# Adding the stored tiles back by blocks of channels, and keeping four tiles on chip

## The chip, the core and the metric

The kernel runs on one core of a Trainium2 chip, as one launch. The metric is the device time in microseconds (us), the median of three runs; beside them stands one execution under the hardware profiler, from which all rows below come. The core's engines are TensorE (PE), VectorE (DVE), ScalarE (ACT), GpSimd (POOL) and SyncE (SP), which here only issues transfers; 16 DMA engines move the bytes.

## What is computed

The output is x + A + B, for 2048 positions (16 tiles of 128) and 448 channels, in 32-bit floats. A is a long causal convolution along the positions, gated by the normalized input; B picks, for each position and each of 16 heads, two of 4096 experts, gathers their rows and sums them.

```
xn = layernorm(x)
# A: a short shift convolution, times v, then a causal convolution as long as the sequence
kv = shift4(k, shift_k) * v
y  = irfft(rfft(kv, 4096) * rfft(ssm_k, 4096))[:2048] + kv * ssm_D
A  = xn * y
# B: scores from xn, the two best experts of each head, a softmax g over them
act = gelu(einsum("nd,nhkd->nhk", xn, u[top_e]))
B   = einsum("nhk,nhk,nhkd->nd", g, act, v[top_e])
out = x + A + B
```

## The kernel before

**Experts.** The 16 position tiles T are worked through in order, each in eight batches, 128 batches in all. A batch is four gathers of 128 rows of 3584 bytes (`gather`, L582, issued by POOL) into one of five slots of `ring`; the product with the position's row on DVE (`prod`, L615, 2 us); four sums on ACT (L621) and a gelu (L623); the coefficients `co` and `cc` (L629, L628), on POOL for the first 104 batches and on DVE for the last 24; and the weighted sum of the four gathered slots on PE into the accumulator `pv` (`val`, L634). After a tile's eighth batch ACT adds the mean and writes the tile from `pv` to the staging tile `fo` (`fold`, L658), and SP stores `fo` to the output (`store`, L662).

**Convolution.** It is a Fourier transform in three steps over groups of four channels. Part 0 holds groups 0 to 27 (channels 0 to 111), part 1 groups 28 to 111 (channels 112 to 447). `conv_in` (L705, L709) transforms to 33 frequencies q; `spectrum` and `inverse` (L756, L773, L801, L820, L824) multiply and go back, frequency by frequency, with the two transforms' real and imaginary columns in `x1b`, a buffer of 84 groups by 33 q by 8 columns. The inverse writes its 17 results over q 0 to 16; the columns of q above 16 are not read again once `spectrum` has read them. `conv_out` ("out0" for part 0, "out1" for part 1) finishes seven groups at a time: seven transposes of `x1b` (`psz`, L842), a copy by ACT (`zt`, L844), seven small matmuls (`fin`, L849) into a PSUM bank, and the gate on DVE, which multiplies by `XA`, the normalized input (L860 for the tiles already done, in place in `XA`; L865 for later ones, into `G`). "out1" has twelve such blocks of 28 channels.

**Why tiles come back.** When tile T is folded before the convolution of its channels is ready, its sum lacks A. "out0" lies behind tile 8 and "out1" behind tile 14. So tiles 0 to 8 lack all of A, and tiles 9 to 14 lack the channels of part 1; tile 15 gets A as a matmul of `G` into `pv` (L652). After the last gate the kernel of before loads tiles 0 to 14 from the output into `x1b` (L1003, from here called read-backs), adds `XA` (L1005, one add per tile) and stores them again (L1006).

**What sets the order.** The program is a list of operations with keys (planned times). A planner in the kernel file (`Plan.solve`) runs a simple model of the engines and takes, on each engine, the ready operation with the lowest key; what it writes out is then the fixed order of each engine. `RANK` is a table that adds, for each kind of operation, four numbers to the keys (interpolated over the kernel's length), and so shifts kinds against each other everywhere. A gather also waits for a PE instruction that the plan put half a us ahead of it. SP issues its transfers strictly in its order.

```python
    join([("x1q", 1, i) for i in range(17)] + ["out_in"], ["fb"])
    for T in range(0, T_OUT1):
        ...
        op("DVE", dve(D - c), lambda T=T, c=c, w=w: nc.vector.tensor_add(second["x1b"][:, w], second["x1b"][:, w], XA[:, T, c:]), ...)
        i = op("SP", 0.08, lambda T=T, c=c, w=w: nc.sync.dma_start(out[T][:, c:], second["x1b"][:, w]), ...)
```

Of the kernel before, what the change touches and what calls it, by code (L numbers as in the profile page):

```python
# [93 lines left out]
class Plan:  # L94
# [133 lines left out]
    "SPwq": (-10.5, 7.5, -46.0, -13.5), "SPx": (92.5, 175.0, 250.5, 125.0), "co": (-183.5, -76.0, -185.5, -457.5),  # L228
    "coef": (-230.5, -356.5, -140.5, -235.5), "ds": (149.0, 210.5, 206.5, 283.0), "es": (64.0, -136.0, 8.5, -185.0),
    "fin@out0": (-90.0, -32.0, -52.5, -95.0), "fin@out1": (-172.5, -183.0, -139.5, -189.5), "flag": (53.5, 83.5, 133.0, 121.0),  # L230
    "fold": (-199.5, -258.0, -262.5, -275.0), "gat": (-151.0, -139.0, 56.5, 85.5), "gate@out0": (-26.0, -26.0, -8.0, -27.5),
    "gate@out1": (-101.5, -201.0, -216.5, -140.0), "gateG@out0": (-31.5, -31.5, -46.0, -85.5), "gateG@out1": (51.5, 33.0, 83.0, 92.0),
# [860 lines left out]
```

## Time and profile before

| what | us |
|---|---|
| median of three runs (906.52, 906.61, 910.87) | 906.61 |
| the profiled execution | 912.46 |
| its span, first to last instruction | 910.7 |
| PE, DVE, ACT, POOL busy | 701.0, 676.3, 569.5, 590.6 |
| mean share of the 16 DMA engines busy by gathers / by SP's transfers | 74.4% / 13.4% |
| last product of the experts (L615) ends | 890.1 |
| last matmul of the transforms (L849) ends | 892.4 |
| read-back adds (L1005) | 893.7 to 901.1 |

The profiled execution lies 5.85 us above the median, 1.75 us of which are outside its span. No engine is busy throughout: the busiest has 77% of the span. In the stretches from 125 to 800 us the DMA engines are busy 84 to 97% and POOL issues a gather every 1.25 us where nothing holds it. The last 20 us look otherwise: the gathers are over, and what runs is the end of the transforms, the adds and the stores. That end is what the change rewrites.

A view of stretches gives, for each stretch of the span, the busy time of each engine (with its instructions), the granted TensorE clock (1.00 is 2.4 GHz, 0.50 is 1.2 GHz), the share of the DMA engines and the GB/s. A timeline row is start, duration, engine, line, operation, tiles and shapes, count, and in brackets the idle time before it with what ended it.

### The profile page before, as it was taken

Reading aid. Unit: us, or ns where it says so; the run is one execution under the profiler, and the core shown is the slowest. Engines: PE = TensorE matmul, PEld = TensorE weight load, DVE = VectorE, ACT = ScalarE, POOL = GpSimd, SP = SyncE. Lnnn points to the kernel's source line nnn. Section 1 sums busy time; section 2 is a strip of 40 time slices with the busy share of each in tenths; the row PEclk is TensorE's granted clock in tenths of the full one; section 3 lists DMA queues with packets and bytes.
Section 4 is the critical chain, followed back from the end, with each engine's and each line's share of the span. In section 5 each row is a group of like instructions: output and inputs, shape, how many; then the busy total and the mean of one; then the engine's idle time right before and its main releaser. Section 6 shows DMA issues by size and latency. Waiting matters only on the chain. (4 is left out here: it accounts for less than half of the span.)

```text
span 910.7 us, 14005 instructions
## 1 busy us (share of the span) xinstructions
PE 701.0 (77%) x4100; PEld 409.5 (45%) x4100; DVE 676.3 (74%) x1577; ACT 569.5 (63%) x1874; POOL 590.6 (65%) x740
## 2 busy tenths in 40 slices
PE   4887786986879868869788865676778878878683
PEld 1434454553545546546456544453433333335451
DVE  2678879878877887787988867667698888874444
ACT  2579764447557656765755666447688887775551
POOL 0156578777776776777777777847777776655630
PEclk9998789998988998998999787778898999996955
DMA  9996688888998998899989899988998999988984
GB/s 370 375 409 235 211 298 282 295 286 297 320 310 293 323 320 272 300 334 311 307 305 350 303 337 326 355 288 280 328 336 301 326 311 341 305 299 278 350 318 150
DMA packets 60054, 280.77 MB, mean 308 GB/s; under 512 B 10304, under 2 KB 21056, under 8 KB 59712
## 3 DMA queue, kind: packets, MB, share of 16 engines
q0 software_dynamic: 40960, 234.91, 74.4%
q1 hardware_dynamic: 19008, 44.87, 13.4%
q8 instruction: 34, 0.56, 0.2%
q14 instruction: 52, 0.43, 0.1%
HBM read 272.98 MB, written 6.77 MB: 307 GB/s over the span
## 5 line engine op out<-in xcount | busy, mean ns | idle before, releaser
L582 POOL DMA_INDIRECT ring<-in_uv_dram,idx x512 | 505.7, 988 | 277.1 <-issue 93.0
L621 ACT ACTIVATE ring<-ring 128x448 f32<-128x448 f32 x512 | 288.7, 567 | 56.6 <-DVE ring L615 29.5
L615 DVE TENSOR_TENSOR ring<-ring,xs 128x1792 f32<-128x1792 f32 x128 | 257.4, 2014 | 71.7 <-DMA ring<-in_uv_dram,idx 50.9
L634 PE MATMUL pv<-ring,cc 128*32 128x448 f32 x1024 | 144.3, 642 | 83.2 <-POOL cc L628 49.4
L482 DVE MAX8 SC<-bank 128x8 f32<-128x64 f32 x512 | 118.6, 232 | 45.7 <-PE bank L477 8.9
L705 PE MATMUL bank<-c,S 128*64 128x132 f32 x896 | 82.8, 340 | 27.2 <-ACT ring L621 12.9
L621 ACT ACTIVATION_READ_ACCUMULATOR ring<-ring 128x1 f32 x512 | 97.2, 190 | 0.0
L473 PE MATMUL bank<-WR,xh 128*128 128x512 f32 x192 | 86.9, 453 | 10.3 <-issue 3.6
L705 PEld LDWEIGHTS bank<-c,S 128*64 128x64 f32 x896 | 66.2, 171 | 62.0 <-ACT ring L621 27.5
L634 PEld LDWEIGHTS pv<-ring,cc 128*32 128x32 f32 x1024 | 21.9, 115 | 133.4 <-POOL cc L628 66.2
L475 PE MATMUL bank<-WR,xl 128*128 128x512 f32 x192 | 78.8, 411 | 0.5 <-DVE xl L462 0.5
L474 PE MATMUL bank<-WR,xh 128*128 128x512 f32 x192 | 78.8, 410 | 0.3 <-DVE WR L432 0.3
L709 ACT ACTIVATE x1b<-bank 128x264 f32<-128x264 f32 x84 | 31.2, 386 | 45.7 <-PE bank L705 38.2
L473 PEld LDWEIGHTS bank<-WR,xh 128*128 128x128 f32 x192 | 38.8, 202 | 41.7 <-issue 15.6
L756 PE MATMUL bank<-x1b,S 128*128 128x336 f32 x132 | 49.9, 489 | 9.1 <-issue 3.9
L489 DVE FIND_INDEX8 SC<-SC,bank 128x8 uint32<-128x256 f32 x128 | 52.5, 423 | 0.0
L688 DVE TENSOR_TENSOR S<-S 128x1024 f32<-128x1024 f32 x28 | 34.6, 1234 | 24.2 <-PE bank L705 16.2
L773 DVE TENSOR_TENSOR S<-bank,S 128x224 f32<-128x224 f32 (+1 forms) x66 | 40.8, 619 | 13.8 <-ACT S L767 6.7
L628 POOL TENSOR_TENSOR cc<-sm,c 128x128 f32<-128x128 f32 x104 | 46.4, 447 | 2.6
L849 PE MATMUL bank<-c,S 128*128 128x64 f32 x168 | 33.2, 357 | 12.9 <-ACT S L844 10.5
L849 PEld LDWEIGHTS bank<-c,S 128*128 128x128 f32 x168 | 29.4, 261 | 29.9 <-ACT S L844 18.5
L475 PEld LDWEIGHTS bank<-WR,xl 128*128 128x128 f32 x192 | 38.1, 199 | 10.3 <-DVE xl L462 1.2
(137 smaller groups left out, 1047.3 us busy)
## 6 DMA issues: line engine op xcount, KB each, us to landing
R<-in_wq_dram SPq DMA_DIRECT2D x16, 896.0 KB
S<-in_kvh_dram SPq DMA_DIRECT2D x28, 400.0 KB
ring<-in_uv_dram,idx POOLq DMA_INDIRECT x512
S<-in_fq_dram SPq DMA_DIRECT2D x32, 128.0 KB
out_dram<-fo SPq DMA_DIRECT2D x16, 224.0 KB
...
```

What stands on the lines that cost most here:

```text
L473: nc.tensor.matmul(o, xh[:, c, :], wh[:, c, ns], start=(c == 0), stop=False)
L474: nc.tensor.matmul(o, xh[:, c, :], wl[:, c, ns], start=False, stop=False)
L475: nc.tensor.matmul(o, xl[:, c, :], wh[:, c, ns], start=False, stop=False)
L482: nc.vector.max(mx[:, 8 * n + j, :] if safe else m2[:, m, 2 * j:2 * j + 8], bank[s.i][:, 64 * j:64 * j + 64])
L489: nc.vector.max_index(m4i[:, 2 * m + g, :], m2[:, m, 8 * g:8 * g + 8], bank[s.i][:, 256 * g:256 * g + 256])
L582: g = nc.gpsimd.indirect_dma_start(dst, None, uv, bass.IndirectOffsetOnAxis(ap=idx[:, T % 8, r, j:j + 1], axis=0)).ins
L615: op("DVE", dve(m * D), lambda: nc.vector.tensor_mul(U[:, :m, :], U[:, :m, :], xs[:, :m, :D]), r=["xs"], w=u[:m], key=k, name="prod")
L621: op("ACT", 0.575, lambda r=r: nc.scalar.activation(U[:, r, :], U[:, r, :], AF.Copy, accum_out=aw[:, r:r + 1]), w=[u[r], ("aw", b % 4, r)] ...
L634: v = nc.tensor.matmul(pv[32 * r:32 * r + 32, :D], cc[b % 3][:, r, :], ring[:, b % RING, r, D:], start=(j == 0), stop=(j == NB - 1), tile_ ...
L705: nc.tensor.matmul(o[64 * i:64 * i + 64, w * j:w * j + w], src, f1[:, i, :], start=True, stop=True, tile_position=(0, 64 * i))
L756: op("PE", 0.95 * n / 448 + 0.05, lambda t=t, sl=sl: nc.tensor.matmul(bank[sl.i][:, :n], fm, x1[p][:, :, q, t, :], start=True, stop=True), ...
L849: nc.tensor.matmul(bank[s.i][:, 64 * j:64 * j + 64], z[:, P * (j - a):P * (j - a) + P], f3, start=True, stop=True)
```

## The change

The read-backs, the adds and the second stores no longer stand behind the last gate.

- `back`: eleven tiles (0 to 10) are loaded from the output into the first 4928 columns of `x1b` as soon as the transposes of the first three blocks of "out1" have read these columns.
- `late`: after every four blocks of "out1" (112 channels) DVE adds that block of channels of the stored tiles into `XA` itself, and SP stores it from `XA`. The first block also takes channels 0 to 111 of tiles 0 to 8. A block of 112 channels of 15 tiles is one add over 11 tiles, one over 4, and one store whose pieces are 112 floats (448 bytes) long.
- `kept`: tiles 11 to 14 are not stored and loaded; `fold` writes them from `pv` into `x1b`, into the columns of q 29 to 32 of groups 28 to 83. For their channels 0 to 111, which were complete, a copy into `XA` comes first.
- `RANK` has new numbers for all kinds, so that the order of every engine changes in detail.

```diff
@@
 T_OUT0, T_OUT1 = 9, 15
+T_KEEP = 11
@@
 RANK = {
-    "late": (2.0, 21.0, 29.0, 29.0), "lateD": (390.5, 125.0, -11.5, 2.0), "mi": (-34.5, -86.5, -17.0, 21.5),
...
+    "late@out1": (189.0, 254.5, 174.5, 99.5), "lateD@out1": (-75.5, -186.0, -122.0, -20.0), "mi": (-431.0, -146.0, 112.5, 268.0),
...
+BACK = 3
@@ fold
+    def kept(a, b):
+
+        m = T_OUT1 - T_KEEP
+        v = second["x1b"].rearrange("p (g q k) -> p q g k", g=84, k=2 * CH)
+        return v[:, 33 - m:, 28 + a // 8:28 + b // 8, :]
+
     def fold(T):
         k = tb(NB * T + NB) + 1.0
+        last = NB * T + NB - 1
+        if T_KEEP <= T < T_OUT1:
+            op("ACT", act(D), lambda: last_val(nc.scalar.activation(kept(0, D)[:, T - T_KEEP], pv[:, :D].rearrange("p (g k) -> p g k", k=2 * CH), AF.Identity, bias=mv[:, T, 0:1]).ins, last),
+               r=[("pv", j) for j in [*range(NB), *more(T)]] + [("psf", 1, q) for q in range(33 - T_OUT1 + T_KEEP, 33)], w=[("fb", T), "pv"], key=k, name="fold")
+            return None, k
@@ ahead of conv_last
+    def back(after, k):
+
+        for T in range(T_KEEP):
+            c = 0 if T < T_OUT0 else 112
+            w = slice(D * T + c, D * T + D)
+            i = op("SP", 0.08, lambda T=T, c=c, w=w: nc.sync.dma_start(second["x1b"][:, w], out[T][:, c:]), w=[("fb", T)], key=k + 0.1 * T, after=(*after, stored[T]), name="SPfb")
+            pl.writer[("fb", T)] = op("DMA", MB * (D - c) / DMA_RATE, None, key=k + 0.1 * T, after=(i,), name="DMAfb")
+
+    def late(a, b, gates, k):
+
+        first = a == 112
+        spans = [(0, T_OUT0, 0), (T_OUT0, T_KEEP, a)] if first else [(0, T_KEEP, a)]
+
+        def into(t0, t1, c):
+            if t0 < T_KEEP:
+                F = second["x1b"][:, :D * T_KEEP].rearrange("p (t d) -> p t d", d=D)
+                nc.vector.tensor_add(XA[:, t0:t1, c:b], XA[:, t0:t1, c:b], F[:, t0:t1, c:b])
+                return
+            x = XA[:, t0:t1, :].rearrange("p t (g k) -> p t g k", k=2 * CH)
+            if first:
+                nc.vector.tensor_copy(x[:, :, 0:14], kept(0, 112))
+            nc.vector.tensor_add(x[:, :, a // 8:b // 8], x[:, :, a // 8:b // 8], kept(a, b))
+        for t0, t1, c in spans + [(T_KEEP, T_OUT1, a)]:
+            n = (t1 - t0) * (b - c)
+            done = op("DVE", dve(n) + (0.63 if first and t0 == T_KEEP else 0.0), lambda t0=t0, t1=t1, c=c: into(t0, t1, c), r=[("fb", t) for t in range(t0, t1)], key=k, after=gates, name="late")
+            c0 = 0 if first and t0 == T_KEEP else c
+            if first or t0 == T_KEEP:
+                u0 = t0 if first else 0
+                i = op("SP", 0.08, lambda u0=u0, t1=t1, c0=c0: nc.sync.dma_start(out[u0:t1].rearrange("t p d -> p t d")[:, :, c0:b], XA[:, u0:t1, c0:b]), key=k + 2.0, after=(done,) if first else (done, ahead), name="SPlate")
...
@@ conv_last
+                gates.append(g)
+                turned.extend(t)
+                if len(gates) == BACK:
+                    back(turned, k + 2.0)
+                if len(gates) % 4 == 0:
+                    b = 112 + CH * done
+                    late(b - 112, b, gates[-4:], k + 4.0)
@@ one_pass
-        stored[T] = store(T, o, k + 1.0, ["fo"])
+        if T < T_KEEP:
+            stored[T] = store(T, o, k + 1.0, ["fo"])
     join(s1_mid, [("zt", i) for i in range(4)])
     conv_last("out1", (1,), T_OUT1, lambda: second["G"])
-    join([("x1q", 1, i) for i in range(17)] + ["out_in"], ["fb"])
...
-        op("DVE", dve(D - c), lambda T=T, c=c, w=w: nc.vector.tensor_add(second["x1b"][:, w], second["x1b"][:, w], XA[:, T, c:]), r=[("x", T)], w=[("fb", T)], key=k + 4.0, name="late")
...
```

Three places of the order show what moved. The first is DVE behind its last product (the last L615). Before:

```order
L615 TENSOR_TENSOR ring<-ring,xs 128x4x448
L629 TENSOR_TENSOR sm<-sm,gat 128x4
L628 TENSOR_TENSOR cc_74<-sm,c_67 128x128
L860 TENSOR_TENSOR XA<-bank_87,XA 128x15x28
L865 TENSOR_TENSOR G<-bank_87,XA 128x28
L629 TENSOR_TENSOR sm<-sm,gat 128x4
L628 TENSOR_TENSOR cc_75<-sm,c_67 128x128
L1005 TENSOR_TENSOR x1b<-x1b,XA 128x336
L1005 TENSOR_TENSOR x1b<-x1b,XA 128x448 x6
```

After (L617 is the product, L631 and L630 the coefficients, L873 and L878 the gates, L948 and L953 the adds of `late`):

```order
L617 TENSOR_TENSOR ring<-ring,xs 128x4x448
L631 TENSOR_TENSOR sm<-sm,gat 128x4
L630 TENSOR_TENSOR cc_74<-sm,c_67 128x128
L948 TENSOR_TENSOR XA<-XA,x1b 128x9x224
L631 TENSOR_TENSOR sm<-sm,gat 128x4
L630 TENSOR_TENSOR cc_75<-sm,c_67 128x128
L873 TENSOR_TENSOR XA<-bank_88,XA 128x15x28
L878 TENSOR_TENSOR G<-bank_88,XA 128x28
L948 TENSOR_TENSOR XA<-XA,x1b 128x2x112
L948 TENSOR_TENSOR XA<-XA,x1b 128x11x112
L873 TENSOR_TENSOR XA<-bank_87,XA 128x15x28
L878 TENSOR_TENSOR G<-bank_87,XA 128x28
```

The first block's large add stands between the last two coefficients, two gates instead of one are behind the last product, and behind the last gate only L948 over 11 tiles and L953 over 4 are left; the other adds over four tiles stand four and seven products earlier.

The second place is PE at the last three `val`. Before, one half block of transforms stands behind the third from last (the first row):

```order
L634 MATMUL pv<-ring,cc_76 32x448 x4
L849 MATMUL bank_87<-c_68,S_72 128x64 x4
L842 MATMUL bank_88<-c_67,x1b 128x128 x3
L849 MATMUL bank_87<-c_68,S_72 128x64 x3
L634 MATMUL pv<-ring,cc_74 32x448 x4
L652 MATMUL pv<-G,c_67 128x336
L634 MATMUL pv<-ring,cc_75 32x448 x4
```

After (L636 is `val`, L862 `fin`, L855 `psz`, L654 the residual):

```order
L636 MATMUL pv<-ring,cc_76 32x448 x4
L862 MATMUL bank_88<-c_68,S_72 128x64 x4
L855 MATMUL bank_87<-c_67,x1b 128x128 x3
L636 MATMUL pv<-ring,cc_74 32x448 x4
L862 MATMUL bank_88<-c_68,S_72 128x64 x3
L855 MATMUL bank_86<-c_67,x1b 128x128 x4
L862 MATMUL bank_87<-c_68,S_72 128x64 x4
L855 MATMUL bank_86<-c_67,x1b 128x128 x3
L862 MATMUL bank_87<-c_68,S_72 128x64 x3
L654 MATMUL pv<-G,c_67 128x336
L636 MATMUL pv<-ring,cc_75 32x448 x4
```

A whole block and half of another now stand behind the last but one `val`; before, nothing of the transforms did.

The third place is SP from the last loads of the spectrum to the end. Before (the two L662 are the stores of tiles 13 and 14):

```order
L344 DMA S_72<-in_fq_dram 128x128
L662 DMA out_dram<-fo 128x448 x2
L1003 DMA x1b<-out_dram 128x336
L1003 DMA x1b<-out_dram 128x448
L1003 DMA x1b<-out_dram 128x336
L1003 DMA x1b<-out_dram 128x448 x4
```

After (L346 are loads, L937 the read-backs, L960 the stores from `XA`, L674 the store of tile 15):

```order
L346 DMA S_72<-in_fq_dram 128x128
L937 DMA x1b<-out_dram 128x448 x4
L937 DMA x1b<-out_dram 128x336
L937 DMA x1b<-out_dram 128x448
L937 DMA x1b<-out_dram 128x336
L937 DMA x1b<-out_dram 128x448 x4
L960 DMA out_dram<-XA 128x4x224
L960 DMA out_dram<-XA 128x9x224
L960 DMA out_dram<-XA 128x2x112
L960 DMA out_dram<-XA 128x15x112 x2
L674 DMA out_dram<-fo 128x448
```

No store stands ahead of the read-backs any more, there are eleven instead of fifteen, and five stores take the place of fifteen.

## Rows read from the trace of the kernel before

**Rows 1.** The page's first line: the span.
```profile
span 910.7 us, 14005 instructions
```
**Rows 2.** Stretches of the last 65 us; the first line names the columns.
```profile
core 0: us, PE busy (x) PEld busy (x) DVE busy (x) ACT busy (x) POOL busy (x), PEclk, DMA share, GB/s
...
838.00:846.00 8.00, 7.42 (x51) 3.94 (x44) 3.08 (x5) 4.78 (x17) 4.72 (x5) 0.78 0.86 277
846.00:862.00 16.00, 10.57 (x79) 7.09 (x78) 6.50 (x11) 8.10 (x25) 9.86 (x11) 1.00 0.97 360
...
866.00:876.00 10.00, 9.19 (x40) 6.61 (x40) 5.06 (x7) 4.54 (x16) 3.78 (x4) 0.50 1.04 400
876.00:888.00 12.00, 10.95 (x49) 6.99 (x50) 4.17 (x10) 6.96 (x22) 4.72 (x5) 0.50 0.76 244
...
902.00:904.00 2.00, 0.00 (x0) 0.00 (x0) 0.00 (x0) 0.00 (x0) 0.00 (x0) 0.50 0.99 365
...
906.00:908.00 2.00, 0.00 (x0) 0.00 (x0) 0.00 (x0) 0.00 (x0) 0.00 (x0) 0.50 0.36 136
```
**Rows 3.** Timeline of the last 27 us: PE, DVE, ACT and SP.
```profile
887.62 1.97 PE L849 MATMUL bank<-c,S 128*128 128x64 f32 x8
888.11 2.02 DVE L615 TENSOR_TENSOR ring<-ring,xs 128x1792 f32<-128x1792 f32 x1 [2.21 <-DMA ring<-in_uv_dram,idx]
889.38 0.85 PE L842 MATMUL bank<-c,x1b 128*128 128x128 f32 x3
...
890.81 1.54 PE L849 MATMUL bank<-c,S 128*128 128x64 f32 x6 [0.58 <-ACT S L844]
...
892.28 1.72 PE L634 MATMUL pv<-ring,cc 128*32 128x448 f32 x8
...
892.38 0.60 DVE L860 TENSOR_TENSOR XA<-bank,XA 128x420 f32<-128x420 f32 x1 [1.85 <-PE bank L849]
...
893.01 0.21 ACT L623 ACTIVATE sm<-sm 128x4 f32<-128x4 f32 x1
...
893.66 7.41 DVE L1005 TENSOR_TENSOR x1b<-x1b,XA 128x336 f32<-128x336 f32 x15
...
897.83 7.62 SPq L1006 DMA_DIRECT2D out_dram<-x1b  x12
```
**Rows 4.** Groups of DVE from 888 us to the end, by shape: busy, mean ns.
```profile
L1005 DVE TENSOR_TENSOR x1b<-x1b,XA 128x448 f32<-128x448 f32 x9 | 5.1, 617 | 0.0
L1005 DVE TENSOR_TENSOR x1b<-x1b,XA 128x336 f32<-128x336 f32 x6 | 2.8, 499 | 0.0
```
**Rows 5.** SP's issues from 700 us, merged: the stores of two tiles, the read-backs.
```profile
806.03 40.70 SPq L662 DMA_DIRECT2D out_dram<-fo  x2
846.84 20.34 SPq L1003 DMA_DIRECT2D x1b<-out_dram  x15
```
**Rows 6.** DVE's waits from 838 to 890 us: total, times, longest.
```profile
DVE ring L615 <- DMA ring<-in_uv_dram,idx: 12.3, 6, 2.8
```
**Rows 7.** PE's timeline from 845 to 866 us, at the full clock.
```profile
845.34 1.10 PE L849 MATMUL bank<-c,S 128*128 128x64 f32 x8
...
847.54 0.88 PE L849 MATMUL bank<-c,S 128*128 128x64 f32 x6 [0.76 <-issue]
848.25 0.61 PE L842 MATMUL bank<-c,x1b 128*128 128x128 f32 x4
...
864.22 0.96 PE L634 MATMUL pv<-ring,cc 128*32 128x448 f32 x8 [2.31 <-DVE ring L615]
```
**Rows 8.** SP's queue, 707 to 748 us: packets, MB, share; what it loaded.
```profile
q1 hardware_dynamic: 720, 0.66, 5.6%
...
S<-in_fq_dram SPq DMA_DIRECT2D x5, 128.0 KB
```
**Rows 9.** The same queue while only stores run, 902 to 904 us.
```profile
q1 hardware_dynamic: 487, 0.73, 98.7%
```
**Rows 10.** POOL's longest stop among its gathers, at 597 us.
```profile
604.90 1.81 POOL L582 DMA_INDIRECT ring<-in_uv_dram,idx  x1 [7.15 <-PE bank L705]
```

More of the change, by code (lines that the diff above doesn't have):

```diff
@@ L221 @@
 RANK = {
[6 rows of a table removed]
[L228 to L232, printed above, removed]
@@ L248 @@
-    "tw@sp1": (129.5, 118.0, 60.5, 76.0), "val": (22.0, -59.5, -110.5, -91.5), "whi": (121.5, 49.0, 75.0, -9.0), "wlo": (99.5, 145.5, 294.5, 154.5),
[3 rows of a table removed]
[6 rows of a table added]
+    "SPx": (580.5, 554.5, 656.0, 575.5), "bad": (12.0, 17.5, -6.0, -6.0), "co": (-640.0, 614.5, -984.0, -1568.5),
+    "coef": (-1188.5, -1812.0, -247.0, -447.5), "ds": (8.0, -4.5, -2.0, 17.0), "es": (150.0, 17.0, -62.5, -174.0),
+    "fin@out0": (-171.0, -51.0, -186.0, 59.5), "fin@out1": (-6.0, 22.5, 0.0, -16.5), "flag": (-3.5, -3.5, -3.5, -3.5),
@@ new lines @@
+    "fold": (-48.0, -16.5, 22.0, 59.5), "gat": (-5.5, -17.0, -12.5, -26.0), "gate@out0": (62.0, -56.0, -23.0, -36.5),
+    "gate@out1": (122.5, -10.0, 63.5, 20.0), "gateG@out0": (-47.5, -53.0, -53.0, -59.0), "gateG@out1": (-122.0, 46.5, 124.5, -16.0),
+    "gather": (491.0, 1036.5, 2680.0, 3056.5), "gelu": (5.5, -167.5, -58.5, 27.5), "hh@sp0": (-12.0, -70.0, -148.5, -100.5),
+    "hh@sp1": (63.5, 29.5, 2.5, -44.5), "idx": (-151.0, -185.5, -143.0, -176.5), "join": (312.5, 248.5, 260.0, 199.0),
[9 rows of a table added]
+    "spread": (-214.5, -109.5, -361.0, -96.0), "stats": (761.5, 890.5, 760.0, 735.5), "store": (118.5, 17.5, 5.5, 20.5),
@@ new lines @@
+    "storeD": (36.5, 36.5, 22.0, 22.0), "sum": (39.5, 16.5, 329.5, 169.0), "tap1@in1": (72.5, 9.5, 123.0, 110.5),
+    "tap2@in0": (-165.5, -276.0, -220.0, -188.0), "tap2@in1": (-6.0, -18.0, -6.0, -6.0), "taps@in0": (63.0, 411.0, 93.5, -59.5),
+    "taps@in1": (-203.0, -197.0, -211.0, -237.5), "th": (332.0, 232.5, 268.5, 132.5), "tw@sp0": (81.5, 95.5, -8.0, 71.0),
+    "tw@sp1": (-24.5, 62.0, 206.0, -19.5), "val": (23.0, -67.5, -71.5, -41.5), "whi": (2.0, 0.0, -14.5, 0.0), "wlo": (97.0, 193.5, 365.5, 341.0),
[3 rows of a table added]
@@ L833, in conv_out @@
         qs = [("x1q", p, i) for i in range(17)]
+        turned = []
         for hf, (a, b) in enumerate([(0, 4), (4, n)]):
@@ L866, in conv_out @@
                w=[("G", p)], key=k, rel=("bank", s), after=(ahead,), name="gateG")
+        return ahead, turned
     norm(0, 1, 1.0)
@@ L916, in conv_mid @@
         pl.stage = ""
+    def back(after, k):
[23 more added lines that the diff above has]
+                i = op("SP", 0.08, lambda u0=u0, t1=t1, c0=c0: nc.sync.dma_start(out[u0:t1].rearrange("t p d -> p t d")[:, :, c0:b], XA[:, u0:t1, c0:b]), key=k + 2.0, after=(done,) if first else (done, ahead), name="SPlate")
+                op("DMA", 1.2 * MB * (b - c0) * (t1 - u0) / DMA_RATE, None, key=k + 2.0, after=(i,), name="lateD")
+            ahead = done
     def conv_last(name, parts, tc0, gv):
@@ L920, in conv_last @@
         tot, done = sum(PARTS[p][1] for p in parts), 0
+        gates, turned = [], []
         for p in parts:
@@ L924, in conv_last @@
                 n = min(7, PARTS[p][1] - c)
-                conv_out(p, c, n, tc0, (gv, off), span(name, done / tot))
+                k = span(name, done / tot)
+                g, t = conv_out(p, c, n, tc0, (gv, off), k)
                 done += n
+                if not p:
+                    continue
+                gates.append(g)
[5 more added lines that the diff above has]
+                    late(b - 112, b, gates[-4:], k + 4.0)
         pl.stage = ""
@@ L994, in one_pass @@
         o, k = fold(T)
-        stored[T] = store(T, o, k + 1.0, ["fo"])
+        if T < T_KEEP:
+            stored[T] = store(T, o, k + 1.0, ["fo"])
     join(s1_mid, [("zt", i) for i in range(4)])
     conv_last("out1", (1,), T_OUT1, lambda: second["G"])
-    join([("x1q", 1, i) for i in range(17)] + ["out_in"], ["fb"])
-    for T in range(0, T_OUT1):
-        c = 0 if T < T_OUT0 else 112
-        k = CONV["out1"][1] + T
-        w = slice(D * T, D * T + D - c)
-        i = op("SP", 0.08, lambda T=T, c=c, w=w: nc.sync.dma_start(second["x1b"][:, w], out[T][:, c:]), r=["fb"], w=[("fb", T)], key=k, after=(stored[T],), name="SPfb")
-        pl.writer[("fb", T)] = op("DMA", MB * (D - c) / DMA_RATE, None, key=k, after=(i,), name="DMAfb")
-        op("DVE", dve(D - c), lambda T=T, c=c, w=w: nc.vector.tensor_add(second["x1b"][:, w], second["x1b"][:, w], XA[:, T, c:]), r=[("x", T)], w=[("fb", T)], key=k + 4.0, name="late")
-        i = op("SP", 0.08, lambda T=T, c=c, w=w: nc.sync.dma_start(out[T][:, c:], second["x1b"][:, w]), r=[("fb", T)], key=k + 4.0, name="SPlate")
-        op("DMA", MB * (D - c) / DMA_RATE, None, key=k + 4.0, after=(i,), name="lateD")
     for T in range(T_OUT1, NT):
```

7 lines of the change are left out of this document (1 added, 6 removed), and 36 rows, old and new, of the table RANK.

## The prediction

> **What bounds the kernel now.** I read the page first, then the stretches of the last 65 us, the timeline of the end, and last the rows of DMA and of waits that give prices. Over the whole span no engine is the bound; gathers and their DMA set the pace of the batches. The span is 910.7 us [rows 1]. The end is another matter. The last product ends at 888.11 + 2.02 = 890.1 us; I call this moment P, since before it the gathers count and after it they don't. From P to the end are 20.6 us [rows 1, 3]. In them the last gate runs at 892.4, the fifteen adds take 893.66 to 901.07, and SP is still issuing stores at 905.45 [rows 3]. The DMA engines are full at 902 to 904 us and have 0.36 of 2 us left after 906, so the last byte goes at about 906.7; from there to the end are 4.0 us [rows 1, 2]. So the tail is a chain: last gate, adds in a row on DVE, 3.3 MB of stores on DMA engines that stood idle for some us before.
>
> Ahead of P the reader is to see two things. The fifteen read-backs are issued from 846.84 to 867.2, behind the store of tile 14 [rows 5], and in just this time the DMA engines go from a share of 0.86 to 0.97 and then 1.04 [rows 2]: the read-backs crowd the gathers. DVE waits 12.3 us for gathers from 838 to 890 us [rows 6]. And TensorE's clock falls to 0.50 (1.2 GHz) behind a stop of PE of 2.31 us for a product [rows 7]; from 866 to 888 us it stays there, with PE busy 20.1 of 22 us [rows 2].
>
> **The change part by part, ahead of P.** Four tiles less are read back: 4 x 0.172 MB = 0.69 MB, at the 400 GB/s of 866 to 876 us [rows 2] 1.7 us. Four tiles less are stored by `fold`: 0.92 MB or 2.3 us of full DMA engines; they lie where the share is 0.86 to 0.97, so I take half, 1.1 us (0 to 2.3). Against that, the first block's store of four tiles (0.46 MB, 1.1 us) now falls among the gathers. The other eleven read-backs move: no store stands before them on SP any more, they wait for the transposes of the third block, which I put 10 us earlier than 846.8. There the DMA engines have 0.14 to spare [rows 2], so 1.4 us of their 6.0 us (2.41 MB at 400 GB/s) are hidden. The bounds are 0 and the 6.0. Sum: 1.7 + 1.1 - 1.1 + 1.4 = 3.1 us; more than the 12.3 us of waits can't be won and nothing may be. So P moves to P' = 887.0 us. `kept` is free: the same ACT instruction with another destination. The copy into `XA` and the two early adds over four tiles cost DVE some 0.6 us each (448 elements, [rows 4]) between products, where DVE waits for gathers anyway; without that cover they cost 1.8 us.
>
> **Behind P.** The amount of adding hardly changes, its place does. Two add sizes [rows 4] give 1.05 ns an element and 0.15 us fixed, so L948 over 9 x 224 takes 2.3 us, over 11 x 112 1.4, L953 0.6. Of the coefficients one pair takes 0.44 us (893.22 to 893.66 [rows 3]).
>
> The stores' price is the unknown: pieces of 448 bytes, of which no row shows one. From below: stores running alone moved 0.73 MB in 98.7% of 2 us x 16 engines [rows 9], 43 ns per 1000 bytes, so 19 ns a piece. From above: the loads of the spectrum, the shortest pieces in the rows, took 5.6% of 41 us x 16 engines for 5 x 128 pieces of 1024 bytes [rows 8], 57 ns, of which bytes explain 44. The 13 ns that remain may be a cost per piece or the crowd of gathers beside them. I take half, 6.5 ns: 26 ns for 448 bytes and 45 ns for 896. Each engine has 72 of the long pieces (nine tiles of 224), 16 (two tiles) and twice 120 (the last two blocks).
>
> Now the timeline from P'. Coefficients 0.44, the large add 2.3, issue and start of the data about 1.1 (905.45 to 906.7 less the last store's own 0.5, plus the issue): data from P' + 3.8, 72 x 45 ns = 3.3, to P' + 7.1. Meanwhile the gelu comes at P + 3.1 [rows 3], coefficients to 3.5, a gate 0.8, the small add 0.4, the second block's 1.4: at 6.2 it is issued, at 7.3 its data run, 120 x 26 ns = 3.1, to P' + 10.4. The third block waits for PE. PE's `val` waits for coefficients at P' + 0.6, and behind it stand a block and a half of transforms: with the full clock `val` 0.96, `fin` x3 0.88, `psz` x4 0.61, the copy's wait 0.58, `fin` x4 1.10, `psz` x3 0.46, 0.58, `fin` x3 0.88 [rows 3, 7], 6.1 us, to P' + 6.7. Then gate 0.9, two adds 2.1, start 1.1: data at P' + 10.8, done at 13.9, tile 15's store 0.6, and 4.0 to the end: P' + 18.5. That is 905.5 us, 5.2 under the span.
>
> The profiled execution took 912.46 us and the median is 906.61; the 5.85 us between are partly outside the span and partly, I think, the clock. I subtract the same 5.2 us: **901.4**.
>
> **What weighs against it.** A measurement of this kernel tells about 0.5% (4.5 us) from no change.
>
> *Half clock.* If PE runs the last blocks at 0.50, as in the rows, the same chain is `val` 1.72, then 1.54, 1.13, 0.58, 1.97, 0.85, 0.58, 1.54: P' + 10.5 instead of 6.7 [rows 3, 7], and the third block and the end move by 3.8 us: 909.3, or 905.2 against the median. For it: the blocks now stand behind `val`s that wait, and it was a wait that came before the fall. Against it: the crowd that made that wait is thinner. The Trainium skill ("TensorE: Matmul & The Clock Gate", Part 1) says that idleness throttles the array and sustained work releases it. By that a PE as busy as from 866 to 888 us would be back at 2.4 GHz, and the forecast's sum would hold; the rows show it was not, so the half clock keeps its chance.
>
> *Slow pieces.* A piece of 448 bytes costs an engine as much as a whole row of 1792 (78 ns by [rows 9]). Then the stores set the end: P' + 7.1, 1.2, twice 9.4, 0.6, 4.0 = P' + 31.7, or 918.7: 8 us longer, 914.6. From 47 ns on (23.7 us less 11.7, over 256 pieces) the change loses, from 65 on by over 0.5%. For it: the time per byte in the short loads is already 30% above the stores'. Against it: those loads ran among gathers. The Trainium skill ("DMA: Bandwidth & Descriptors", Specifications) states that transfers under 512 B fall off line rate because the DMA engine reads, modifies and writes. By that rule the stores would be this rival, 914.6; no row here shows such a piece of data, and the 16 small packets of each transfer are no store of this kind.
>
> *Another order elsewhere.* `RANK` rewrites the order of all 128 batches. What that can cost is seen at 597 us: gathers stand still for 7.15 us because they keep pace with PE, which has five blocks of `conv_in` in a row [rows 10]. The new order has these five in a row too. One such stop more gives 908.6, two give 916, one less 894.2. Counted from product to product, the two orders differ nowhere by more than some one block of `conv_in` or ten matmuls of `spectrum` (L756), so I expect no net stop, but the rows can't exclude one.
>
> *It does not do what it says.* If the read-backs still come late, as when the third block is delayed, P' = P and the full clock gives 904.5: within 0.5%; I count it with the half clock.
>
> **Numbers.** Forecast 42% (of it 32 faster, 10 same); half clock and late read-backs 22% (5, 15, 2 slower); slow pieces 15% (2 same, 13 slower); order 21% (7, 5, 9). Faster by over 0.5% 0.44, within 0.32, slower 0.24. The range goes from the forecast with the read-backs wholly hidden and one short stop less, 895, to just under the slow pieces, 913; about 8 in 100 lie below and 12 above.
>
> **What would show it.** The last product should end near 887 us of a like span, with DVE's waits for gathers in its last 50 us under 12; read-backs should be issued some 10 us earlier. Behind the last gate there should be two adds and one issue, and under 13 us to the end. SP's queue in the last 15 us gives the price of the short pieces: near 26 ns I am right, above 47 the tail is longer than before. The granted clock over the last twelve blocks tells full from half. And products per 25 us from 100 to 800 should be as before; if they aren't, the order elsewhere decides, and my sum is of the wrong place.

## The result, and the profile after

The change takes 912.17 us in the median against 908.34 for the kernel before, 20 runs each: ratio 1.0046, interval [1.0027, 1.0066]. A second comparison (below) gave 1.0011 [0.9982, 1.0040]. The forecast was 901.4 against 906.61, 0.6% faster. So it failed in sign: the change is 0.5% slower in the first comparison, inside the range 895 to 913 and near its upper end, and not to be told from before in the second. The ratios of all comparisons leave out the runs that are over 1.5% above the fastest of the same kernel: none in this first one, but 3 of 12 of b2, 2 of 6 of the first x1, and 3 of 6 of b5, 5 of 12 of x5 and 12 of 19 of before in the last one.

The two traces taken alone say the opposite. Before's execution took 912.46 us, as long as the slowest of its 20 runs (912.40); the one of the change took 908.72, and 13 of its 20 runs were slower. The span, and the stretches of the end (columns as in [rows 2]):

```profile
span 906.9 us, 13959 instructions
```
```profile
812.00:836.00 24.00, 19.32 (x101) 12.43 (x103) 11.12 (x18) 13.56 (x45) 12.83 (x14) 0.64 0.94 330
836.00:846.00 10.00, 7.92 (x57) 3.98 (x49) 3.91 (x7) 5.98 (x19) 6.49 (x7) 0.84 1.03 375
846.00:862.00 16.00, 14.20 (x80) 9.39 (x80) 8.36 (x13) 9.31 (x30) 8.78 (x10) 0.69 0.90 324
...
870.00:885.00 15.00, 12.55 (x57) 8.19 (x56) 7.63 (x11) 7.43 (x25) 4.99 (x6) 0.50 0.71 236
```

The DMA engines are full at 836 to 846 us, where in before they had 0.14 to spare [rows 2]; in exchange the share at 846 to 862 falls from 0.97 to 0.90. DVE's waits for gathers in the 52 us ahead of the last product are not shorter (12.3 us in [rows 6]):

```profile
DVE ring L617 <- DMA ring<-in_uv_dram,idx: 14.2, 7, 3.7
```

SP's issues show the read-backs (L937), then the block stores (L960):

```profile
811.85 23.71 SPq L937 DMA_DIRECT2D x1b<-out_dram  x11
843.52 54.47 SPq L960 DMA_DIRECT2D out_dram<-XA  x5
```

The end, in the timeline of PE, DVE, ACT and SP (start, us, engine, line):

```profile
883.52 2.02 DVE L617 TENSOR_TENSOR ring<-ring,xs 128x1792 f32<-128x1792 f32 x1 [0.59 <-DMA ring<-in_uv_dram,idx]
...
884.64 1.97 PE L862 MATMUL bank<-c,S 128*128 128x64 f32 x8
...
886.30 2.26 DVE L948 TENSOR_TENSOR XA<-XA,x1b 128x2016 f32<-128x2016 f32 x1 [0.35 <-issue]
886.41 0.85 PE L855 MATMUL bank<-c,x1b 128*128 128x128 f32 x3
...
887.19 1.72 PE L636 MATMUL pv<-ring,cc 128*32 128x448 f32 x8
888.58 9.40 SPq L960 DMA_DIRECT2D out_dram<-XA  x4
888.84 1.42 PE L862 MATMUL bank<-c,S 128*128 128x64 f32 x6
...
891.39 1.10 PE L862 MATMUL bank<-c,S 128*128 128x64 f32 x8 [0.69 <-ACT S L857]
...
893.40 1.54 PE L862 MATMUL bank<-c,S 128*128 128x64 f32 x6 [0.58 <-ACT S L857]
894.99 0.59 DVE L873 TENSOR_TENSOR XA<-bank,XA 128x420 f32<-128x420 f32 x1 [2.36 <-PE bank L862]
...
895.61 1.44 DVE L948 TENSOR_TENSOR XA<-XA,x1b 128x1232 f32<-128x1232 f32 x1
...
896.97 0.62 DVE L953 TENSOR_TENSOR XA<-XA,x1b 128x448 f32<-128x448 f32 x1
...
899.60 0.38 SPq L674 DMA_DIRECT2D out_dram<-fo  x1
```

The last product ends at 885.5 (P'), and from it to the end of the span are 21.4 us, where before had 20.6 [rows 1, 3]. The adds are where they were foreseen (2.26, 1.44 and 0.62 us), but they come late. PE still has transforms at the half clock when the last product ends (1.97 us for eight matmuls, 1.10 at the full clock), so that the last but one `val` starts at P' + 1.65 instead of P' + 0.6; it and the block and a half behind it end at 894.9, with 1.72, 1.42 and 1.54 us near or at the half clock and 1.10 at the full one. I call the time from the end of the last product to the end of the span the **tail**. In two traces of one program it differed by at most 1.4 us (before, 20.6 and 19.1), and what of it lies behind the last gate by at most 0.5, while the totals of one kernel in one comparison are 7 to 24 us apart. So one trace gives a measure of the end, as it doesn't of the total.

### The profile page after: what moved, and what is told of

Read it like the earlier page. It is cut to its first block, busy times and chain, and to the rows that moved or that the text cites. A ratio compares the mean times of both kernels' runs of the same rounds, so it can differ in the third digit from the quotient of the medians.

```text
span 906.9 us, 13959 instructions
## 1 busy us (share of the span) xinstructions
PE 696.1 (77%) x4100; PEld 408.3 (45%) x4100; DVE 673.2 (74%) x1570; ACT 570.1 (63%) x1874; POOL 593.1 (65%) x740
## 4 chain that ended last, share of the span: by engine, by line
PE 40%; DVE 15%; issue 15%; POOL 12%; DMA 8%; ACT 6%; another core or an unknown queue 2%; SPq 0%; DVEq 0%; POOLq 0%; ACTq 0%
POOL ring L584 9%; PE pv L636 7%; DMA ring<-in_uv_dram,idx 5%; DVE SC L484 4%; PE bank L717 4%; DVE ring L617 4%; PE bank L862 4%; PE bank L475 4%; PE bank L811 3%; PE bank L476 3%; PE bank L477 3%; ACT ring L623 3%; DMA S<-in_kvh_dram 2%; PE bank L855 2%
## 5 line engine op out<-in xcount | busy, mean ns | idle before, releaser
L617 DVE TENSOR_TENSOR ring<-ring,xs 128x1792 f32<-128x1792 f32 x128 | 256.9, 2013 | 67.7 <-DMA ring<-in_uv_dram,idx 57.6
L636 PE MATMUL pv<-ring,cc 128*32 128x448 f32 x1024 | 140.2, 626 | 72.0 <-POOL cc L630 37.2
L717 PE MATMUL bank<-c,S 128*64 128x132 f32 x896 | 76.6, 323 | 35.0 <-issue 12.1
L475 PE MATMUL bank<-WR,xh 128*128 128x512 f32 x192 | 89.2, 464 | 18.5 <-ACT zt L857 4.2
L717 PEld LDWEIGHTS bank<-c,S 128*64 128x64 f32 x896 | 61.9, 162 | 66.6 <-ACT ring L623 24.2
L477 PE MATMUL bank<-WR,xl 128*128 128x512 f32 x192 | 81.5, 424 | 1.1 <-DVE xl L464 1.1
L476 PE MATMUL bank<-WR,xh 128*128 128x512 f32 x192 | 82.3, 428 | 0.0
L636 PEld LDWEIGHTS pv<-ring,cc 128*32 128x32 f32 x1024 | 21.7, 113 | 125.2 <-issue 61.5
L475 PEld LDWEIGHTS bank<-WR,xh 128*128 128x128 f32 x192 | 40.2, 209 | 47.4 <-issue 13.2
L785 DVE TENSOR_TENSOR S<-bank,S 128x224 f32<-128x224 f32 (+1 forms) x66 | 40.6, 618 | 19.9 <-ACT S L779 6.9
L630 POOL TENSOR_TENSOR cc<-sm,c 128x128 f32<-128x128 f32 x104 | 47.1, 453 | 2.5
L779 ACT ACTIVATE S<-bank 64x112 f32<-64x112 f32 x132 | 33.9, 257 | 21.6 <-PE bank L764 11.7
L477 PEld LDWEIGHTS bank<-WR,xl 128*128 128x128 f32 x192 | 40.4, 210 | 11.7 <-DVE xl L464 1.9
L476 PEld LDWEIGHTS bank<-WR,xh 128*128 128x128 f32 x192 | 40.6, 211 | 7.0
```

What stands on the lines that cost most here:

```text
L475: nc.tensor.matmul(o, xh[:, c, :], wh[:, c, ns], start=(c == 0), stop=False)
L476: nc.tensor.matmul(o, xh[:, c, :], wl[:, c, ns], start=False, stop=False)
L477: nc.tensor.matmul(o, xl[:, c, :], wh[:, c, ns], start=False, stop=False)
L617: op("DVE", dve(m * D), lambda: nc.vector.tensor_mul(U[:, :m, :], U[:, :m, :], xs[:, :m, :D]), r=["xs"], w=u[:m], key=k, name="prod")
L630: last_val(ve.tensor_mul(cc[b % 3], co[:, :, None].broadcast_to([P, 4, 32]), rep[:, None, :].broadcast_to([P, 4, 32])).ins, b - 3)
L636: v = nc.tensor.matmul(pv[32 * r:32 * r + 32, :D], cc[b % 3][:, r, :], ring[:, b % RING, r, D:], start=(j == 0), stop=(j == NB - 1), tile_ ...
```

## Experiments

The theories: **TAIL**, the loss lies behind the last product (half clock, short stores); **EARLY** or **CROWD**, the moved read-backs cost the gathers more than they did; **ORDER**, the rewritten table of ranks costs somewhere else. In "the old order" the change runs with the ranks of before: the new operations cost nothing in the plan, so that POOL and, but for one matmul, PE execute the list of before, and the new instructions are only put in between.

**Change without new order (e1), new order without change (e2), no short stores (e3), before again (b2).**

```diff
 e1, in the change
-RANK = {... as rewritten ...}
+RANK = {... of before; the five new kinds as in the change ...}
-op("DMA", MB * (D - c) / DMA_RATE, ..., name="DMAfb")   # and dve(n) of "late", the cost of "lateD"
+op("DMA", 0.0, ..., name="DMAfb")
 e2, in before
-RANK = {... of before ...}
+RANK = {... as rewritten; the old names of the moved kinds as in before ...}
 e3, in the change
-lambda u0=u0, t1=t1, c0=c0: nc.sync.dma_start(out[u0:t1] ...
+lambda u0=u0, t1=t1, c0=c0: None if not first else nc.sync.dma_start(out[u0:t1] ...
```

> The change in the order of before: the table of ranks is that of before, and the planner counts the new operations at zero, so that PE, POOL and ACT run the whole list of before and the read-backs, adds and block stores are only put in between. Theory ORDER (the change itself brings about what its sum says, and the rewritten table takes it away elsewhere): faster than before by 3 to 6 us, ratio 0.993 to 0.997, and the last product near 4 us earlier than in a trace of before. Theory TAIL (the last blocks at half clock, behind the last waits, and the short store pieces eat more than the gathers gain): as slow as the change, ratio 1.003 to 1.007. Theory EARLY (the read-backs and adds, moved among the gathers, cost the gathers there more than they give): ratio 1.003 to 1.007 too, but with the last product not earlier than in a trace of before.

> The rewritten table of ranks alone, with read-backs, adds and stores at the end as before. ORDER: slower than before by more than the change is, 6 to 10 us, ratio 1.006 to 1.011. TAIL and EARLY: the order costs nothing, ratio 0.998 to 1.002.

> The changed kernel without the stores of the last two blocks of channels (they are left out, the output is incomplete; the adds stay). TAIL: what the change loses lies in these stores and what waits behind them, so 3 to 4 us come back: ratio to before 0.999 to 1.001. ORDER and EARLY: the store of tile 15, which stands 0.6 us behind the last gates' fold, then sets the end; 1 to 2 us come back, ratio 1.002 to 1.004.

> The kernel before once more, for a second trace of it and for the scatter of the comparison: ratio 0.998 to 1.002 by every theory; the times of the batches in its trace tell which of the differences between the first two traces are the kernels' and which an execution's.

Measured: e1 1.0004 [0.9974, 1.0034], e2 1.0197 [1.0150, 1.0244], e3 1.0024 [0.9992, 1.0056], and before against itself 0.9960 [0.9923, 0.9997], with medians of 864.86 and 864.79 us. The last one sets the scale: differences under 0.4% between two of these comparisons are not told apart here. e1 lies in the range of none of the theories, and the interval of e3 overlaps those of all.

e2 costs 17 us, far over what ORDER had given. Its trace shows where (start, us, engine, line):

```profile
840.94 2.02 DVE L615 TENSOR_TENSOR ring<-ring,xs 128x1792 f32<-128x1792 f32 x1 [2.71 <-DMA ring<-in_uv_dram,idx]
...
858.21 0.59 DVE L860 TENSOR_TENSOR XA<-bank,XA 128x420 f32<-128x420 f32 x1 [5.65 <-PE bank L849]
...
858.84 7.42 DVE L1005 TENSOR_TENSOR x1b<-x1b,XA 128x336 f32<-128x336 f32 x15
```

The last gate runs 15 us after the last product (2.25 us in before, 9.5 in the change), and all fifteen adds stand behind it: tail 33.4 us. So the new order is no order for the old kernel: it puts transforms behind the products because blocks can be added singly, and the two parts of the change can't be priced one by one.

e1 is the other half: in the old order the change's tail is 14.7 us, but the last product ends 3.0 us later than in the trace of before from the same chip (849.7 against 846.7). The trace shows one place for it, in DVE's waits of the 100 us ahead of the last product and in DVE's timeline:

```profile
DVE ring L617 <- DMA ring<-in_uv_dram,idx: 26.4, 9, 6.2
DVE XA L948 <- DMA x1b<-out_dram: 7.1, 1, 7.1
```
```profile
800.48 2.56 DVE L948 TENSOR_TENSOR XA<-XA,x1b 128x2016 f32<-128x2016 f32 x2 [7.07 <-DMA x1b<-out_dram]
802.95 2.02 DVE L617 TENSOR_TENSOR ring<-ring,xs 128x1792 f32<-128x1792 f32 x1
```

The add over nine tiles stood in front of a product before its data were there. In before's trace (b2) the waits for gathers in the like 100 us are 30.4 us, so the two kinds of e1 together are 3.1 us more. e3 gains nothing that can be told. Its end comes 10.2 us behind the last gate, against 11.9 and 12.0 in the two traces of the change: the short stores cost some 1.7 us of the tail.

**The adds later (e5), the change again (a2), and each order for one part (s1, s2).** In e5 the first block's adds wait for the seventh gate; s1 and s2 execute one order up to batch 112 and the other behind it.

```diff
 e5, in e1
-if len(gates) % 4 == 0:
+if len(gates) in (7, 8, 12):      # the first block's adds at 7
 ...
```

> As e1 (the change in the order of before), but the first block's adds are put three gates later on DVE (behind the seventh gate, not the fourth): in e1 DVE stood still for 7.1 us in front of the add over nine tiles, for the read-backs, with a product queued behind it. Theory STOP (that wait is what took the gain away in e1): 4 to 7 us faster than before, ratio 0.992 to 0.996, no wait of DVE for read-backs, the last product 3 to 6 us earlier than in e1. Theory CROWD (the read-backs take the gathers' DMA time, wherever DVE waits for it): as e1, ratio 0.998 to 1.002, and the 7 us turn up as waits of DVE for gathers.

> The changed kernel once more, beside the others: ratio 1.002 to 1.007 if its loss is the kernel's own; 0.998 to 1.001 if it hung on the chip of the first runs.

> The changed kernel with its own order for the first 112 of the 128 batches and, behind them, the order of e5. Theory TAIL ORDER (the new order loses at the end, where it leaves a block and a half of transforms behind the last products): as e5, ratio 0.992 to 0.996. Theory HEAD ORDER (it loses somewhere in the first 112 batches): as the change, ratio 1.002 to 1.007.

> The other way round: the order of before for the first 112 batches and that of the change behind them. TAIL ORDER: as the change, ratio 1.002 to 1.007. HEAD ORDER: as e5, ratio 0.992 to 0.996.

Measured, on one chip: e5 1.0010 [0.9979, 1.0041], a2 1.0011 [0.9982, 1.0040], s1 1.0052 [1.0021, 1.0082], s2 1.0043 [1.0010, 1.0076]. DVE's wait for read-backs is gone from e5, and the time is that of before: STOP fell, CROWD's number came. CROWD's sign, the 7 us as waits for gathers, is seen in one trace of e5 and not in the other (32.0 and 23.4 us, 26.4 in e1). a2 lies between its two forecasts. s1 and s2 are both slower, while a2, which has both of the parts that they have singly, is not: neither HEAD ORDER nor TAIL ORDER says that, and differences of this size are at the scatter. What the four show firmly is the tail, in one trace each: 14.6, 21.9, 14.3 and 20.5 us. Among these four it goes with the order of the end.

**Without read-backs (x1, x2), and with late ones (x3).**

```diff
 x1, in before, and x2, in e5
-lambda T=T, c=c, w=w: nc.sync.dma_start(second["x1b"][:, w], out[T][:, c:])
+lambda: None
 x3, in e5
-if len(gates) == BACK:
-    back(turned, k + 2.0)
+if len(gates) == 5:
+    held = op("SP", ..., lambda: nc.sync.dma_start(out[15][0:1, 0:4], XA[0:1, 0, 224:228]), after=(g,))
+    back([*turned, held], k + 2.0)
-if len(gates) in (7, 8, 12):
+if len(gates) in (10, 11, 12):
```

> The kernel before without its fifteen read-backs (they are left out: the adds run on what stands in the tile, the output is wrong there); the order is untouched. Theory PLACE (in the last 55 us PE, at half clock, sets the pace of the gathers, so DMA given back there gains nothing): ratio 0.997 to 1.001. Theory BYTES (their 3.10 MB take the gathers 6 to 8 us wherever they lie): ratio 0.991 to 0.994.

> e5 (the change in the old order, first adds behind the seventh gate) without its eleven read-backs (left out, the output is wrong there). In e5 they lie 83 to 60 us ahead of the last product's end, in before 43 to 23 us ahead of it. PLACE: out there gathers do set the pace, so 4 to 6 us come free and the gain of the tail is seen: ratio to before 0.992 to 0.996. BYTES: 5 to 6 us come free too, 0.993 to 0.996, but then x1 gains as much. If neither x1 nor x2 gains, the read-backs cost nothing and the loss ahead of the last product is something else.

> e5 with the read-backs held back on SP to the fifth gate (by a store of 16 bytes in front of them that reads what this gate writes, and that tile 15's store overwrites), so that they lie some 45 to 25 us ahead of the last product as in before, and the adds of the first block behind the tenth gate, those of the second behind the eleventh. PLACE: the 4 to 6 us come back and both kernels are beaten: ratio 0.993 to 0.997, tail 14 to 17 us. BYTES: as e5, 0.998 to 1.003.

Measured, on another chip: x1 0.9891 [0.9825, 0.9956], x2 0.9938 [0.9903, 0.9974], x3 0.9911 [0.9877, 0.9945]. x3 computes all and is as fast as x2, which reads nothing back. That looked like PLACE, but x1 gains too, which PLACE excluded. So I put the question to the changed kernel itself, and repeated the three that matter together:

```diff
 x4, in the change: the order on SP alone
+moved = [o for o in order if o.name == "SPfb"]     # the eleven read-backs
+order = [o for o in order if o.name != "SPfb"]
+hold = Op()
 ...
+n = order.index(hold_at[4]) + 1                    # behind the fifth gate
+order[n:n] = [hold, *moved]
```

> The changed kernel in its own order on PE, DVE, ACT and POOL; only on SP the read-backs are held back to the fifth gate, as in x3. PLACE: 3 to 5 us faster than the change, ratio to before 0.995 to 1.000, the rest of what x3 gains being lost by the block and a half behind the last products. If the place of the read-backs matters in the old order only: as the change, 1.001 to 1.005.

> x3 once more: 0.988 to 0.995 if it beats both kernels on any chip; 0.997 or more if the first result was the chip's.

> e5 once more, beside x3 on one chip; they differ in the place of the read-backs and of the first two blocks' adds alone. PLACE: 0.997 to 1.003, and slower than x3 by 0.005 to 0.009. If x3's gain was the chip's: no difference beyond 0.003.

> Before without its read-backs once more (left out, the adds run on what stands in the tile, the output is wrong there). PLACE: 0.997 to 1.001. BYTES: 0.991 to 0.994.

Measured, again on another chip: x4 1.0095 [1.0062, 1.0127], x3 0.9980 [0.9949, 1.0011], e5 0.9998 [0.9965, 1.0031], x1 0.9966 [0.9937, 0.9994]. PLACE falls: late read-backs don't help the change in its own order (x4 is above the ranges of both theories), and in the old order they gain 0.2% on this chip, which can't be told from nothing. x1 gives the price: all fifteen read-backs, 3.10 MB, cost before 0.34% [0.06, 0.63], some 3 us and at most 5.7, and not the 7.8 us that they take at 400 GB/s [rows 2]. The first x1 gave 1.1% [0.44, 1.75], from four runs, which doesn't exclude 7.8. The two intervals overlap from 0.4 to 0.6%; 3 to 5 us is my estimate from both.

The chains of e5 and x3 behind the last product, the first of e5, the second of x3 from the same chip:

```profile
884.62 2.02 DVE L617 TENSOR_TENSOR ring<-ring,xs 128x1792 f32<-128x1792 f32 x1 [1.93 <-DMA ring<-in_uv_dram,idx]
...
889.45 1.44 DVE L948 TENSOR_TENSOR XA<-XA,x1b 128x1232 f32<-128x1232 f32 x1
...
894.33 0.34 SPq L674 DMA_DIRECT2D out_dram<-fo  x1
```
```profile
882.87 2.02 DVE L617 TENSOR_TENSOR ring<-ring,xs 128x1792 f32<-128x1792 f32 x1 [4.00 <-DMA ring<-in_uv_dram,idx]
...
885.83 1.44 DVE L948 TENSOR_TENSOR XA<-XA,x1b 128x1232 f32<-128x1232 f32 x1
...
890.86 0.34 SPq L674 DMA_DIRECT2D out_dram<-fo  x1
```

The last block's adds are 2.8 us behind the product's end in e5 and 0.9 in x3; the tails are 14.6 (901.2 less 886.6) and 12.1 us (897.0 less 884.9). Part of this is no gain: in x3 the last product waited 4.00 us for its gathers, the transforms were done meanwhile, and the last gate runs right behind it.

**The clock: stops of PE filled (b5, x5, a5).**

```diff
 in before, x3 and the change
+def fill(n):
+    for _ in range(n if opened[0] else 0):
+        nc.tensor.matmul(pv[:64, :128], ident[:64, 64:], c1[:64, 0:128], start=False, stop=False)
 def val():
+    if LATE <= b < 126:
+        fill(8)
+    opened[0] = j < NB - 1
 ...
 def fin(...):
+    if p:
+        fill(1)
```

> The kernel before with work added on PE alone: in front of the products with the gathered values of batches 104 to 125 (where they would wait) eight matmuls on a block of zeros, added to the sum that is open, and one in front of each half of the last transforms; nothing of the result changes. In the trace of before a stop of PE of some 3 us is followed by a granted clock of 0.50 for up to 30 us, with PE busy 2.00 of 2 us. Theory CLOCK: with the stops filled the mean granted clock of the last 100 us ahead of the last product rises from 0.77 to 0.82 to above 0.9, and 3 to 6 us are gained: ratio 0.993 to 0.997. Rival FILL: the clock stays and the added work, some 20 us of PE, is partly in the way: ratio 1.002 to 1.015.

> x3 (the change in the old order, read-backs late) with the same fill. CLOCK: 3 to 6 us faster than x3, ratio to before 0.985 to 0.994, clock above 0.9. FILL: slower than x3, 0.998 to 1.01.

> The changed kernel with the same fill. CLOCK: the chain behind the last product runs at the full clock, as the forecast had it, and stops ahead of it cost less: 4 to 8 us faster than the change, ratio 0.993 to 1.000. FILL: slower than the change, 1.006 to 1.02.

Measured, on one chip: b5 1.0130 [1.0063, 1.0197], x5 1.0025 [0.9984, 1.0065], a5 1.0132 [1.0078, 1.0185]. The first stretch in each fence is the 100 us ahead of the last product, the second the 10 us behind it; the third number from the right is the granted clock. The change, then a5:

```profile
785.50:885.50 100.00, 77.79 (x414) 46.01 (x415) 56.87 (x91) 59.57 (x187) 55.35 (x59) 0.77 0.89 307
885.50:895.50 10.00, 8.18 (x44) 5.74 (x43) 5.98 (x12) 4.12 (x12) 0.00 (x0) 0.67 0.60 167
```
```profile
754.00:854.00 100.00, 96.58 (x701) 65.76 (x701) 59.07 (x94) 61.39 (x195) 57.09 (x60) 0.98 0.90 319
854.00:864.00 10.00, 8.40 (x53) 4.46 (x51) 7.95 (x14) 4.01 (x12) 0.00 (x0) 0.83 0.63 170
```

The clock rose as CLOCK said, from 0.77 to 0.98, and all three times lie in FILL's ranges. The fill was too large to decide what a rise of the clock alone is worth ahead of the last product: 37.5 us of PE in a5 where I had reckoned 20, so that PE was busy 96.6 of 100 us. But behind the last product, where little fill stands, a5 runs the chain at the full clock:

```profile
852.00 2.02 DVE L623 TENSOR_TENSOR ring<-ring,xs 128x1792 f32<-128x1792 f32 x1 [2.02 <-DMA ring<-in_uv_dram,idx]
...
854.48 0.96 PE L645 MATMUL pv<-ring,cc 128*32 128x448 f32 x8 [0.27 <-DVE cc L636]
...
857.74 1.10 PE L873 MATMUL bank<-c,S 128*128 128x64 f32 x8 [0.33 <-ACT S L866]
...
859.76 0.88 PE L873 MATMUL bank<-c,S 128*128 128x64 f32 x6 [0.22 <-ACT S L866]
...
860.68 0.59 DVE L884 TENSOR_TENSOR XA<-bank,XA 128x420 f32<-128x420 f32 x1 [0.89 <-PE bank L873]
```

The last gate starts at P' + 6.7, and the tail is 19.0 us. In the change the gate starts at P' + 9.5.

| the end of the kernel, in us | last gate behind the last product | end behind the last gate | tail |
|---|---|---|---|
| before: b2, before, x1 twice | 0.3, 2.3, 2.2, 2.0 | 18.8, 18.3, 17.6, 18.0 | 19.1, 20.6, 19.8, 20.1 |
| the change's order and operations: the change, a2, s2, x4 | 9.5, 10.0, 8.2, 8.3 | 11.9, 12.0, 12.2, 11.9 | 21.4, 21.9, 20.5, 20.1 |
| the same without the short stores: e3 | 10.6 | 10.2 | 20.8 |
| its operations in the old order: e1, e5 twice, s1, x2 | 2.4, 2.3, 2.2, 2.4, 2.4 | 12.3, 12.3, 12.4, 11.9, 12.3 | 14.7, 14.6, 14.6, 14.3, 14.7 |
| the same, first adds later still: x3 twice | 0.3, 0.3 | 11.8, 11.8 | 12.1, 12.1 |
| its order alone: e2 | 15.3 | 18.2 | 33.4 |
| with fill: b5, a5, x5 | 0.3, 6.7, 0.3 | 18.5, 12.3, 12.3 | 18.9, 19.0, 12.7 |

The two columns separate the two parts: the change's operations take some 6 us from what stands behind the last gate, in either order, and its order puts the last gate 8 to 10 us behind the last product (6.7 at the raised clock).

## Why the prediction was wrong, point by point

Two steps failed: the choice of the full clock for the chain behind the last products, which the prediction itself prices at 3.8 us, and P' = P - 3.1, the gain ahead of them.

**The tail, right in its parts and wrong in the clock.** Forecast was P' + 18.5 at the full clock and P' + 22.3 at the half one. The change has 21.4 and 21.9; a5, with the clock raised, has 19.0, with three pairs of fill of 0.43 us in the chain, partly inside the waits for the copy. Its last gate starts at P' + 6.7, as forecast. In a2, where the clock is 0.50 in the 10 us behind the last product, the gate starts at P' + 10.0, against 10.5 in the forecast for the half clock. Behind the gate the change and a2 need 11.9 and 12.0 us, where 11.8 were forecast. So the sum holds at either clock, and the step that failed is the choice of the full clock as the likelier. The rows spoke against it [rows 2, 7]. The trace of the change, first a row of PE's timeline, then stretches of 4 us:

```profile
821.20 1.26 PE L636 MATMUL pv<-ring,cc 128*32 128x448 f32 x8 [3.29 <-DVE sm L631]
```
```profile
818.00:822.00 4.00, 0.80 (x8) 0.16 (x8) 2.99 (x5) 1.73 (x6) 3.09 (x4) 0.97 0.99 339
822.00:826.00 4.00, 3.19 (x16) 2.39 (x13) 0.99 (x1) 1.79 (x6) 1.50 (x3) 0.50 0.98 367
826.00:830.00 4.00, 4.00 (x19) 2.22 (x20) 2.05 (x5) 2.90 (x10) 2.88 (x3) 0.50 0.84 256
...
834.00:838.00 4.00, 4.00 (x23) 1.70 (x22) 1.15 (x4) 1.96 (x7) 2.03 (x4) 0.50 1.00 334
838.00:842.00 4.00, 4.00 (x36) 2.33 (x29) 1.96 (x2) 1.12 (x2) 2.82 (x3) 0.90 1.03 396
```

PE stands nearly still at 818 to 822, and from 822 to 838 the clock is 0.50, with PE busy 14.6 of 16 us. The thinner crowd didn't prevent it. The stop came where the moved read-backs fill the DMA engines (a share of 0.99): PE waited 3.29 us for DVE's coefficients, and the product ahead of these had waited 3.83 us for its gather. The rule of the Trainium skill that I weighed ("TensorE: Matmul & The Clock Gate", Part 1) has sustained work release the throttle. b5 and a5 agree in one point, that work put into the stops keeps the clock near 1.00 (1.00 and 0.98 over 100 us); the rows from 822 to 838 us, with PE busy and the clock at 0.50, don't bear it out.

**P' = P - 3.1, wrong.** By the totals less the tails (21.7 us for the change and 19.9 for before, in the mean) the last product came 2.4 us later than before's in the first comparison and 0.8 earlier in the second, each with 2 to 3 us of uncertainty. The term was made of bytes at 400 GB/s, and of 1.4 us for the moved read-backs. x1 shows that such bytes cost 1.0 to 1.6 us per MB here (by the estimate of 3 to 5 us for 3.10 MB), not the 2.5 that I took. By that price the 0.69 MB less of read-backs, 0.92 less of stores and 0.46 more, 1.15 MB in all, are worth 1.2 to 1.8 us; the forecast, which had halved the stores, has 1.7, so that this part was hardly off. The 1.4 us are not seen in the rows: the read-backs came 35 us earlier (811.85 against 846.84), not 10, into a stretch which they fill in their turn. But x4, where they come late, isn't faster, so what their place is worth is not shown. DVE's waits for gathers, foreseen under 12 us, are 14.2. The trace's own P' of 885.5, 4.6 under before's, is no proof for the step: a block more of transforms now stands behind it, and the executions differ. The traces, one each, point to the place: from the 112th product to the last the change takes 99.1 and 98.7 us (a2), and before 95.2; e3 takes 93.6 and b2, on the same chip, 88.5. So the last sixteen batches are some 4 to 5 us longer, where 3.1 were to be gained. Which of the moved transfers, the adds and the clock costs them stays open.

**The price of short pieces, nearly right.** SP's queue at 890 to 892 us, where long pieces of 896 bytes run, and at 896 to 898 and 898 to 900, where those of 448 do:

```profile
q1 hardware_dynamic: 681, 0.61, 98.1%
```
```profile
q1 hardware_dynamic: 520, 0.23, 58.3%
...
q1 hardware_dynamic: 792, 0.35, 73.5%
```

98.1% of 32 us over 681 packets are 46 ns (45 forecast); 58.3% over 520 and 73.5% over 792 are 36 and 30 ns (26 forecast), under the 47 from which the change would have lost by it. The Trainium skill's rule ("DMA: Bandwidth & Descriptors", Specifications), by which pieces under 512 B fall off line rate, is seen in a small measure: 66 to 80 ns per 1000 bytes against 51 for the long pieces and 43 for whole rows [rows 9].

**Another order elsewhere, not where I looked.** Products per 100 us in the stretches from 400 to 600 us (DVE's busy time and count), before and then after:

```profile
400.00:500.00 100.00, 31.83 (x17) 0.91 0.92 319
500.00:600.00 100.00, 26.75 (x14) 0.80 0.94 334
```
```profile
400.00:500.00 100.00, 31.79 (x17) 0.90 0.90 311
500.00:600.00 100.00, 27.08 (x14) 0.88 0.92 325
```

No net stop is seen there, and in no stretch of 100 us from 100 to 800 do the counts differ by more than 2. What the new order does is at the end: with the same operations it makes the tail 20.1 to 21.9 us where the old order has 14.3 to 14.7. On one chip the total doesn't show it (a2 at 1.0011, e5 at 1.0010), and I take it that the same transforms then stand ahead of the last product and are paid there; no run shows that by itself. On another it does: x4, in the new order, is at 1.0095, and x3 and e5, in the old one, at 0.9980 and 0.9998. As far as these pairs tell, the order costs between nothing and 1%.

**The sum.** Forecast -5.2 us; measured +3.8 in one comparison and some +1 in the other, so 6 to 9 us are missing. The tail accounts for 3.2 (21.7 in the mean of the change's two traces for 18.5), nearly all of it ahead of the last gate, where the chain hangs on PE's clock; before's tail accounts for 0.7 (19.9 in the mean for the 20.6 that I set out from), and the price of bytes and the 1.4 us for 1.3 to 1.9. The rest, up to 4 us, stays open; it lies ahead of the last product. s1 and s2 place 0.3 to 0.4% in the order of either part, a2 doesn't bear them out, and the interval of each is as large.

**A version that may beat both.** x3 was faster than before on one chip, 0.9911 [0.9877, 0.9945], and not to be told from it on another, 0.9980 [0.9949, 1.0011]; both lie below the change's 1.0046 and 1.0011, but x3 and the change were not timed on the same chip.
